# Where a step of a sliding-window attention copies the next query, and what stands ahead of it

## The chip, the core and the metric

The kernel runs on one core of one Trainium2 chip, in float32 throughout, with the matrix products split into high and low parts. The metric is the device time of one execution in microseconds (us), lower being better. Five engines work side by side and each takes its instructions strictly in the order in which they were issued: TensorE (PE in the profile; its weight loads are PEld), VectorE (DVE), ScalarE (ACT), GpSimd (POOL) and SyncE (SP), which issues nearly all DMAs. What one engine needs from another it waits for by a semaphore, and everything queued behind a waiting instruction on the same engine waits with it.

## The reference

Four layers with a residual each, on one sequence of 2048 rows of 640 values: attention, Fourier mixing, attention, Fourier mixing. An attention layer has 32 heads of 20 values; each row looks at 8 rows, itself and every second one before it. Cut to what matters:

```python
def _A_ref(x, wqkv, wo):                     # H = 32, Dh = 20, W, dil = 8, 2
    qkv = (x @ wqkv).reshape(B, S, 3, H, Dh).transpose(2, 0, 3, 1, 4)
    q, k, v = qkv[0], qkv[1], qkv[2]
    idx = pos[:, None] - arange(W)[None, :] * dil            # masked where < 0
    logits = einsum("bhsd,bhswd->bhsw", q, k[idx]) * Dh ** -0.5
    attn = softmax(where(mask, logits, -1e9))
    o = einsum("bhsw,bhswd->bhsd", attn, v[idx])
    return o.transpose(0, 2, 1, 3).reshape(B, S, D) @ wo

x = x + _A_ref(layernorm(x), wqkv, wo)
x = x + Real(DFT_seq(DFT_hidden(layernorm(x))))              # as matrix products
x = x + _A_ref(layernorm(x), wqkv, wo)
x = x + Real(DFT_seq(DFT_hidden(layernorm(x))))
```

## The kernel before, in words

`layer_a` is one attention layer and runs twice; `LayerB` is a Fourier layer. This case is about `layer_a`. The sequence is cut into 4 chunks c of 512 rows (128 partitions of 4 rows j), the heads into 8 groups e of 4 heads. A unit u = (c, e), 32 of them, is one head group on one chunk. A window of 8 rows and 20 values per head is too small for TensorE, so logits and weighted sums are made elementwise on VectorE and GpSimd, while TensorE makes the q, k, v projections of the following chunk, the output projections of the chunk before, and the first products of the Fourier layer.

The layer is written as steps, two to a unit: unit u's two halves (jp = 0 and 1, two rows each) start in the even step 2u and the odd step 2u + 1. A helper `at(step, phase, fn)` files every piece of work under a step and a phase name; at the end the list `PHASES` gives the order of the phases inside a step, and all pieces are issued in that order, for all five engines at once and without any other scheduler. So `PHASES` alone decides who stands behind whom on an engine within a step. Different phases may hold work of different engines; only the order among those of one engine, and the waits between engines, matter.

The pieces that matter here, by step:

- `qk` (`qk_mul`, L421 on DVE and L423 on POOL), each step: products of query and window, 128x1280 values, then POOL adds the two halves of each head.
- `red0`, `red1` (`qk_red`, L429 on DVE): the rest of the logit sum, one step after its `qk`. `red0` is the second half's and falls into even steps, `red1` the first half's and falls into odd steps.
- `qc` (`q_copy`, L394 on ACT), odd steps: copies the next unit's query from the landed tile `qs` into `qp`, in PSUM. There is one `qp`.
- `sA`, `sB`, `sC` (L444, L446, L448 on DVE), then `exp` (L437 on ACT), in even steps: mask, maximum, subtraction, exponential of the unit before.
- `sD`, `sE`, `sF` (L450, L452, L454 on DVE), odd steps: sum, reciprocal, and the probabilities `pp`.
- `av0`, `av1` (`av_mul`, L459 on DVE; `av_tree`, L474 to L476 on POOL): probability times value window, and a tree of adds. `av0` falls into even, `av1` into odd steps.
- ACT also empties the projections' PSUM banks: `evac`, `evacA`, `evacO` (L359), splits transposed tiles into high and low parts (`hi` L321, `actL` L340), and does `actl`: normalisation of x (L172, L181), its statistics (L141 to L160, first layer), output statistics (L154 to L160), the high part of wo (L550), the Fourier layer's input (L181, L843).
- PE: transposes (`peT0`, L317), projections (`pe`, `pe2`, L352), subtraction of the high part (`peL`, L325), output projections (L499), Fourier products (`pe3`, L886).
- POOL: `fin`, the reciprocal root of a variance (L164, L166). SP: `dma` with the query's load (`q_load`, L386, L391) and `dma2` with loads for the Fourier layer (L185, L485, L486).

`qp`, the probabilities `pp`, the maximum `mx`, the sum `sm` and the mask all are parts of one PSUM tile `pq` (2 KB a partition). Waits are made for the tile as a whole, so the query copy waits for the last access of VectorE to any part of it that was issued ahead of the copy, and a later write of VectorE to `sm` waits for the copy.

```python
        pq = pt([P, 512], "pq")
        qp = pq[:, : NJ * FE].rearrange("p (j f) -> p j f", j=NJ)
```

Of the kernel before, what the change touches and what calls it, by code (L numbers as in the profile page):

```python
# [71 lines left out]
def tile_layers(ctx: ExitStack, tc: tile.TileContext, x, wqkv, wo, cs, wre, wim, out):  # L72
# [159 lines left out]
    def layer_a(li, stats, handoff, prev):  # L232
# [545 lines left out]
        for z in range(len(thirds) // 3):  # L778
# [8 lines left out]
        at(63, "misc", handoff.c_lo, 13)  # L787

        PHASES = (
            "peT0 dma evac hi pe peL pe2 fin red0 dma2 qk sA sB av0 sD red1 sE sC exp evacA actL evacO actl sF av1 qc"  # L790
            " dmaw dmas misc dmac dmar pe3w pe3"
        ).split()
        with tc.manual_schedule(engines=ENGINES):
# [425 lines left out]
    st0 = [None] * NC  # L1219
    b1, b2 = LayerB(1), LayerB(3)  # L1220
    layer_a(0, st0, b1, None)
    st2 = [None] * NC
    b1.run(st2)
    layer_a(2, st2, b2, b1)
    b2.run(None)
    b2.ytile(NT - 1, 0, None)
# [56 lines left out]
```

## Time and profile before

| | us |
|---|---|
| median of 3 runs | 1844.46 |
| lowest and highest run | 1843.17, 1844.85 |
| the profiled execution | 1844.03 |
| its span, first to last instruction | 1842.2 |

| engine | busy us | share of the span |
|---|---|---|
| PE | 1762.7 | 96% |
| DVE | 1443.5 | 78% |
| ACT | 821.8 | 45% |
| POOL | 716.4 | 39% |

The two attention layers take, roughly, 30 to 370 us and 950 to 1310 us of the span. How to read the rows: a group's row has the line, engine, operation, tiles, count, then busy time and the mean of one in ns, then the idle time of the engine just ahead of the group and what ended most of it. A row of the timeline has the start in us from the span's start, the duration, the engine, the line and the tiles, and in brackets how long the engine was idle ahead of it and who released it. A row of the windows has, for each stretch, the busy time of PE, PEld, DVE, ACT and POOL, then the granted TensorE clock, the share of the DMA engines and the rate in GB/s. A row of the waits has who waited for whom, the total, the number of times and the longest.

### The profile page before, as it was taken

How to read it: one execution, taken by the hardware profiler on the slowest of the kernel's cores; microseconds unless marked ns; L12 is line 12 of the kernel's file. 1: busy time of each engine (PE TensorE's matmuls, PEld its weight loads, DVE VectorE, ACT ScalarE, POOL GpSimd, SP SyncE). 2: the span in 40 equal slices, each digit the busy share in tenths (PEclk: the TensorE clock that was granted, in tenths of full speed). 3: DMA queues.
4: the chain of work that ended last, by engine and by line, in shares of the span. 5: the costliest groups of instructions: out<-in, count | busy, mean ns of one | idle time of the engine just before them, and what ended most of it. 6: DMA issues, size and time to landing. Idle time of an engine off the chain costs nothing.

```text
span 1842.2 us, 26541 instructions
## 1 busy us (share of the span) xinstructions
PE 1762.7 (96%) x8798; PEld 1517.6 (82%) x8798; DVE 1443.5 (78%) x2158; ACT 821.8 (45%) x1713; POOL 716.4 (39%) x637
## 2 busy tenths in 40 slices
PE   9999997988999999999998999988889999999999
PEld 7789896767788888888897798977678888888888
DVE  5899899989867767767649988898798676676673
ACT  5554544553445444445624334445533443443441
POOL 4799898954200000000028987889441000000000
PEclk9999998999999999999999999989999999999999
DMA  6766677656777687676646665775477776876861
GB/s 232 227 188 212 190 229 240 208 173 230 246 261 242 207 272 234 221 261 220 190 145 220 217 198 180 218 263 187 158 248 246 262 242 205 273 238 217 262 216 51
DMA packets 261722, 401.89 MB, mean 218 GB/s; under 512 B 21808, under 2 KB 146224, under 8 KB 261328
## 3 DMA queue, kind: packets, MB, share of 16 engines
q1 hardware_dynamic: 258384, 398.22, 66.9%
q10 hardware_dynamic: 3200, 1.97, 0.3%
q8 instruction: 70, 1.15, 0.3%
q14 instruction: 68, 0.56, 0.1%
HBM read 326.63 MB, written 73.47 MB: 217 GB/s over the span
## 4 chain that ended last, share of the span: by engine, by line
PE 66%; DVE 16%; DMA 5%; issue 5%; POOL 5%; ACT 3%; SPq 0%; DVEq 0%; ACTq 0%; POOLq 0%
PE m L352 15%; PE aux L964 12%; PE t L1054 10%; PE m L1054 10%; PE pq L1054 5%; PE xt L1054 5%; PE aux L499 5%; DVE pr L421 3%; DVE pr L459 2%; DMA win<-cs_in 1%; POOL pr L474 1%; DVE s L1016 1%; DVE s L1017 1%; DVE lg L429 1%; POOL pr L423 1%
## 5 line engine op out<-in xcount | busy, mean ns | idle before, releaser
L352 PE MATMUL m<-r,s 128*128 128x480 f32 x1920 | 442.0, 385 | 9.7 <-ACT stg L359 4.2
L352 PEld LDWEIGHTS m<-r,s 128*128 128x128 f32 x1920 | 358.0, 190 | 67.0 <-ACT stg L359 6.5
L1047 ACT CAST r<-win 128x512 fp32r<-128x512 f32 x242 | 147.9, 621 | 176.6 <-DVE win L1083 91.4
L964 PE MATMUL aux<-r2a,zo 128*128 128x320 f32 x768 | 226.3, 309 | 0.0
L474 POOL TENSOR_TENSOR pr<-pr 128x640 f32<-128x640 f32 x126 | 205.0, 1627 | 49.9 <-DVE pr L459 49.3
L164 POOL TENSOR_TENSOR stats<-stats,mhalf 128x1 f32<-128x1 f32 (+1 forms) x40 | 27.6, 689 | 490.0 <-ACT stats L160 489.9
L421 DVE TENSOR_TENSOR pr<-pq,win 128x1280 f32<-128x1280 f32 x128 | 189.8, 1483 | 33.0 <-ACT pq L394 33.0
L964 PE MATMUL aux<-pr,zo 128*128 128x320 f32 x704 | 208.0, 309 | 0.0
L1048 DVE TENSOR_TENSOR r<-win,r 128x512 fp32r<-128x512 f32 x242 | 162.6, 687 | 42.1 <-ACT r L1047 40.9
L459 DVE TENSOR_TENSOR pr<-pq,win 128x1280 f32<-128x1280 f32 x128 | 190.9, 1491 | 4.5 <-DVE pq L454 0.2
L423 POOL TENSOR_TENSOR pr<-pr 128x640 f32<-128x640 f32 x128 | 184.7, 1443 | 19.7 <-DVE pr L421 16.3
L1054 PE MATMUL m<-r,r 128*128 128x512 f32 x600 | 154.5, 392 | 0.0
L886 PE MATMUL m<-s,r 128*128 128x512 f32 x384 | 123.7, 410 | 27.2 <-DVE s L871 13.9
L964 PEld LDWEIGHTS aux<-r2a,zo 128*128 128x128 f32 x768 | 144.1, 188 | 2.0
L964 PEld LDWEIGHTS aux<-pr,zo 128*128 128x128 f32 x704 | 132.2, 188 | 2.2
L1054 PE MATMUL t<-r,r 128*128 128x512 f32 x492 | 133.5, 393 | 0.0
L1054 PEld LDWEIGHTS m<-r,r 128*128 128x128 f32 x600 | 112.5, 188 | 25.1 <-DVE r L1048 0.3
L886 PE MATMUL t<-s,r 128*128 128x512 f32 x384 | 121.8, 405 | 2.5 <-DVE ot L943 2.0
L475 POOL TENSOR_TENSOR pr<-pr 128x320 f32<-128x320 f32 x126 | 118.7, 942 | 9.9
L886 PEld LDWEIGHTS m<-s,r 128*128 128x128 f32 x384 | 71.3, 193 | 51.0 <-DVE s L871 20.1
L359 ACT COPY stg<-m 128x480 f32<-128x480 f32 x128 | 71.0, 556 | 94.9 <-PE m L352 85.0
L1083 DVE TENSOR_TENSOR win<-win,win 128x512 f32<-128x512 f32 x109 | 74.9, 690 | 47.6 <-DMA win<-cs_in 46.2
(271 smaller groups left out, 3455.7 us busy)
## 6 DMA issues: line engine op xcount, KB each, us to landing
win<-cs_in SPq DMA_DIRECT2D x348, 256.0 KB, 3.9
r<-xc SPq DMA_DIRECT2D x240, 256.0 KB, 4.2
win<-kvb SPq DMA_DIRECT2D x96, 440.0 KB, 3.9
xa<-cs_in SPq DMA_DIRECT2D x120, 256.0 KB, 3.7
win<-kvb SPq DMA_DIRECT2D x64, 360.0 KB, 4.2
xc<-stg SPq DMA_DIRECT2D x40, 512.0 KB, 3.6
kvb<-stg SPq DMA_DIRECT2D x60, 320.0 KB, 4.3
xr<-xs SPq DMA_DIRECT2D x40, 320.0 KB, 3.1
```

The lines of the kernel that those rows point to most:

```text
L352: nc.tensor.matmul(mt[g][:, : 3 * F], st[:, a, k], wq[q][:, b, k], start=n == 0, stop=n == 14)
L421: nc.vector.tensor_tensor(pr, q, wview(u, jp, 0, [[1, FE]]), op=ALU.mult)
L423: nc.gpsimd.tensor_tensor(pv[:, :, 0:10], pv[:, :, 0:10], pv[:, :, 10:20], op=ALU.add)
L459: nc.vector.tensor_tensor(pr.rearrange("p j w (h d) -> p j w h d", d=DH), lgs[u][:, 2 * jp : 2 * jp + 2].unsqueeze(4).to_broadcast([P, 2, ...
L474: g.tensor_tensor(pr[:, :, 0:4], pr[:, :, 0:4], pr[:, :, 4:8], op=ALU.add)
L475: g.tensor_tensor(pr[:, :, 0:2], pr[:, :, 0:2], pr[:, :, 2:4], op=ALU.add)
L499: nc.tensor.matmul(m[:, :320], oT[(c, j)][:, a, k], wo_s["w"][:, b, k, e * 320 : (e + 1) * 320], start=(i, k) == (0, 0), stop=(i, k) == (2 ...
L886: self.last = nc.tensor.matmul(self.z[t][k], self.xn[c][:, a, j, k * P : (k + 1) * P], self.ct[s][:, b], start=s == 0 and i == 0, stop=s = ...
L964: self.last = nc.tensor.matmul(self.ym[e][:, :320], zt[(k, a, ri)][:, j2 * P : (j2 + 1) * P], w[:, e * 320 : (e + 1) * 320], start=(k, a, ...
L1047: nc.scalar.copy(hi, raw)
L1048: nc.vector.tensor_tensor(lo, raw, hi.bitcast(F32), op=ALU.subtract)
L1054: nc.tensor.matmul(bank, w(a, kb), hl[b], start=start and (a, b) == (0, 0), stop=stop and (a, b) == (1, 0),)
```

## The change

Only the order of the phases changes. `red0`, `dma2`, `qk`, `qc` and `red1` go to the head of the step, in that order; the rest keeps its order.

```diff
         PHASES = (
-            "peT0 dma evac hi pe peL pe2 fin red0 dma2 qk sA sB av0 sD red1 sE sC exp evacA actL evacO actl sF av1 qc"
+            "red0 dma2 qk qc red1 peT0 dma evac hi pe peL pe2 fin sA sB av0 sD sE sC exp evacA actL evacO actl sF av1"
             " dmaw dmas misc dmac dmar pe3w pe3"
         ).split()
```

No instruction is added or removed. Engine by engine, in the order in which they are issued:

- PE: nothing moves.
- DVE: in each odd step the logit sum L429 (`red1`) goes ahead of the sum L450 (`sD`). Nothing else moves.
- ACT: in each odd step the query copy L394 goes from the end of the step to its beginning: ahead of `evac`, `hi`, `evacO` and `actl` of that step, but still behind all of the even step before. The copy now follows the second query product of its step and no longer the probability product (L459).
- POOL: `fin` goes behind L423 of the same step.
- SP: the query's load goes behind the loads of `dma2`, on 12 steps.
- Waits: the copy's target is in `pq`, so L450, which is issued behind the copy now, waits for it, and the first query product of the next unit (L421) has no wait for ScalarE left.

## The prediction

> **What bounds the kernel now.** I read the page first, then the busy time by stretches, then the table of waits, and last the timeline of single steps.
>
> ```profile
> PE 1762.7 (96%) x8798; PEld 1517.6 (82%) x8798; DVE 1443.5 (78%) x2158; ACT 821.8 (45%) x1713; POOL 716.4 (39%) x637
> ...
> L421 DVE TENSOR_TENSOR pr<-pq,win 128x1280 f32<-128x1280 f32 x128 | 189.8, 1483 | 33.0 <-ACT pq L394 33.0
> ```
>
> PE is busy nearly throughout, but as an average over stages. The second row is what the change is about: 128 products, two to a query copy, and VectorE stood 33.0 us in all ahead of them. The stretches of the two attention layers tell where that can count:
>
> ```profile
> 75.00:113.00 38.00, 33.88 (x142) 27.52 (x140) 36.57 (x46) 15.10 (x38) 31.62 (x29) 0.91 0.61 195
> 113.00:225.00 112.00, 111.63 (x590) 99.53 (x591) 101.99 (x142) 62.57 (x163) 102.04 (x98) 1.00 0.67 207
> 225.00:285.00 60.00, 59.01 (x320) 52.76 (x318) 54.37 (x83) 27.79 (x67) 56.26 (x52) 1.00 0.72 221
> 285.00:362.00 77.00, 63.80 (x312) 55.20 (x313) 70.26 (x100) 37.61 (x91) 69.59 (x62) 0.91 0.67 220
> ...
> 1036.00:1180.00 144.00, 144.00 (x765) 129.04 (x764) 123.89 (x178) 60.76 (x152) 122.86 (x113) 1.00 0.65 206
> 1180.00:1290.00 110.00, 96.40 (x501) 84.75 (x501) 97.84 (x145) 52.56 (x128) 100.32 (x88) 0.94 0.68 220
> ```
>
> From 113 to 225 and from 1036 to 1180 PE has next to no gap (111.63 of 112, 144 of 144): there a VectorE that waits costs nothing until the stretch ends. In 75 to 113 VectorE is busy 36.57 of 38 us and PE only 33.88: VectorE leads. From 225 on VectorE and GpSimd carry the end of the layer together (54.37 and 56.26 of 60, then 70.26 and 69.59 of 77), while PE has 13 to 14 us of gaps in each last stretch. So the change is worth what it does to VectorE and GpSimd where they take over from PE, about 225 and 1180, and what it does to PE where PE takes over, about 113 and 1016.
>
> ```profile
> ACT pq L394 <- DVE pr L459: 37.4, 21, 4.7
> DVE pr L421 <- ACT pq L394: 33.0, 21, 4.8
> ```
>
> The copy waited 37.4 us for the probability product, with all later work of ScalarE behind it; that goes. VectorE's 33.0 us came in 21 places. The Trainium skill ("Perfetto Trace Analysis", Optimization Strategy) says that a gap which repeats for a stretch can mean too few SBUF or PSUM buffers for the next tile. By it the gap would not go away here, since there is still one query buffer; the rival of no change below is what that would make.
>
> **The wait that takes its place.** In the changed order the sum L450 is a write to the copy's PSUM tile that stands behind the copy, and so waits for it; the next unit's L421 no longer does. The copy itself has left behind the ScalarE work of its own odd step, but not that of the even step: bank eviction, low parts, normalisation for the Fourier layer. VectorE therefore meets the copy about 3.7 us earlier in its own list (L450, L452, L454, L459 and a logit sum come after the new place and came before the old). The pair of steps at 1178 shows it:
>
> ```profile
> 1178.60 1.49 DVE L421 TENSOR_TENSOR pr<-pq,win 128x1280 f32<-128x1280 f32 x1
> 1179.10 0.32 ACT L437 ACTIVATE lg<-lg 128x128 f32<-128x128 f32 x1
> 1180.18 0.38 DVE L450 TENSOR_REDUCE pq<-lg 128x16 f32<-128x128 f32 x1
> 1180.48 0.81 DVE L429 TENSOR_REDUCE lg<-pr 128x64 f32<-128x640 f32 x1
> 1181.20 0.26 DVE L452 RECIPROCAL pq<-pq 128x16 f32<-128x16 f32 x1
> 1181.49 0.29 DVE L454 TENSOR_TENSOR pq<-lg,pq 128x128 f32<-128x128 f32 x1
> 1181.82 1.49 DVE L459 TENSOR_TENSOR pr<-pq,win 128x1280 f32<-128x1280 f32 x1
> 1181.97 0.56 ACT L359 COPY stg<-m 128x480 f32<-128x480 f32 x1 [2.55 <-PE m L352]
> 1182.43 0.76 ACT L340 CAST ot<-t 128x256 fp32r<-128x256 f32 x2
> 1183.06 0.94 ACT L181 ACTIVATE xa<-xa,stats 128x640 f32<-128x640 f32 x1
> 1183.39 1.58 POOL L474 TENSOR_TENSOR pr<-pr 128x640 f32<-128x640 f32 x1 [1.17 <-DVE pr L459]
> 1184.04 0.73 ACT L843 CAST r<-xa 128x640 fp32r<-128x640 f32 x1
> 1186.07 0.42 ACT L394 COPY pq<-qs 128x320 f32<-128x320 f32 x1
> 1186.52 1.49 DVE L421 TENSOR_TENSOR pr<-pq,win 128x1280 f32<-128x1280 f32 x1 [2.48 <-ACT pq L394]
> ```
>
> L359, L340, L181 and L843 are of the even step and stay ahead of the copy; L359 there waits for a projection on PE. L843 ends at 1184.77, so the copy runs 1184.79 to 1185.21 (0.9 us earlier than now), L450 starts at 1185.24, L452 at 1185.65 instead of 1181.20: 4.45 later. L421 loses its wait of 2.48. Net the next unit starts 4.45 - 2.48 = 1.97 us later, and L474 on GpSimd, released by L459, 4.4 later, where it had 1.17 of idle time. Queued behind the waiting L450 is all of VectorE's step; GpSimd waits for that.
>
> Where ScalarE has only short work ahead of the copy, the move is free: the copy needs 0.06 + 0.42 + 0.03 = 0.5 us from the end of the step's L421 (gaps between neighbouring rows), and L429, now ahead of L450, covers it with 0.72 (1180.48 to 1181.20). The cover is gone once ScalarE is over 0.2 us late. Such pairs are most.
>
> **Leaving PE's stretch, layer one.**
>
> ```profile
> 223.61 1.49 DVE L421 TENSOR_TENSOR pr<-pq,win 128x1280 f32<-128x1280 f32 x1
> 226.24 0.26 DVE L452 RECIPROCAL pq<-pq 128x16 f32<-128x16 f32 x1
> 227.94 0.79 ACT L340 CAST ot<-t 128x256 fp32r<-128x256 f32 x2
> 230.46 1.49 DVE L421 TENSOR_TENSOR pr<-pq,win 128x1280 f32<-128x1280 f32 x1 [1.39 <-ACT pq L394]
> ...
> 246.75 0.25 DVE L452 RECIPROCAL pq<-pq 128x16 f32<-128x16 f32 x1
> 247.56 0.73 ACT L843 CAST r<-xa 128x640 fp32r<-128x640 f32 x1
> 250.04 1.49 DVE L421 TENSOR_TENSOR pr<-pq,win 128x1280 f32<-128x1280 f32 x1 [0.46 <-ACT pq L394]
> ```
>
> The same working: L340 ends at 228.73, the copy at 229.17, L452 starts at 229.6 instead of 226.24, 3.37 late, less 1.39: 1.98. At 247 L843 ends at 248.29, L452 would start at 249.17: 2.4 late, less 0.46. That is 1.96 by itself, but a VectorE that already is 2.0 late finds the first part of ScalarE's list done. Laid behind its exponential, the list (0.32, 0.56, 0.76, 0.94, 0.73 and the copy's 0.42, less 0.1 of overlap between neighbours) takes about 3.2 against 2.2 for L421 and L429: about 1 us more. Later pairs with a normalisation in the even step would cost 1 us each again, but GpSimd is the later one there. Sum: 3.1 late (2.0 + 1.1). Layer two: 1.97 at 1178 and, by the same list, 1.5 in the pair behind it: 3.5.
>
> **What comes back.** In the ends of the layers some waits lie behind work that the copy does leave (odd steps' casts, statistics, normalisation):
>
> ```profile
> 345.52 1.49 DVE L421 TENSOR_TENSOR pr<-pq,win 128x1280 f32<-128x1280 f32 x1 [0.82 <-ACT pq L394]
> 1247.38 1.49 DVE L421 TENSOR_TENSOR pr<-pq,win 128x1280 f32<-128x1280 f32 x1 [1.32 <-ACT pq L394]
> ```
>
> 0.8 in layer one, 1.3 in layer two.
>
> **Where PE takes over.**
>
> ```profile
> 113.78 1.48 DVE L421 TENSOR_TENSOR pr<-pq,win 128x1280 f32<-128x1280 f32 x1
> 114.00 0.93 ACT L181 ACTIVATE xa<-xa,stats 128x640 f32<-128x640 f32 x1
> 116.70 0.60 PE L317 MATMUL xt<-ident,xa 128*128 128x128 f32 x4
> ...
> 1010.26 1.48 DVE L421 TENSOR_TENSOR pr<-pq,win 128x1280 f32<-128x1280 f32 x1
> 1015.04 0.43 ACT L394 COPY pq<-qs 128x320 f32<-128x320 f32 x1 [5.21 <-issue]
> 1015.41 0.55 ACT L359 COPY stg<-m 128x480 f32<-128x480 f32 x1
> 1016.01 2.37 PE L352 MATMUL m<-r,s 128*128 128x480 f32 x8 [2.32 <-ACT stg L359]
> ```
>
> At 113.78 the copy now stands ahead of an eviction and of the normalisation L181, and waits for L421's end at 115.26. Copy, eviction and bias behind it, L181 ends at about 117.45; the transposes that started at 116.70 start 0.8 later. At 1016 the opposite: ScalarE stood 5.21 us at the copy with an eviction behind it for which PE waited 2.32. The copy can now run at 1011.8, and these 2.32 go; but a normalisation that moves behind the copy soon after takes most of it back, by the row at 114. Bounds 0 and 2.32 of gain; I take 0.4, nearer to the lower, since VectorE leads up to there.
>
> **What moves at no cost.** PE's order does not change. On VectorE L450 and L452 become neighbours that depend on each other: 0.02 a pair (0.38 + 0.03, and 0.72, against 1.1 now), 1.2 us over 62 pairs if all were on the path, under half of it. The Trainium skill ("VectorE: DVE Perf Modes", The DRAIN you can't avoid) says that a semaphore between chained operations costs nothing extra: 0 by it; I take 0. On GpSimd the 0.55 us roots (L164) go behind L423; their reader is a step later, so nothing waits; without that cover 0.55 each. On SP the query's load goes behind up to two loads of `dma2` on 12 steps; it can be issued a pair of steps ahead of its use, and without that cover costs its place in the queue.
>
> **Sum.** +0.8 + 3.1 - 0.8 - 0.4 + 3.5 - 1.3 = +4.9 us on the profiled execution's 1844.03 (1842.2 of span and 1.8 around): 1848.9. The median of the runs is 0.4 above that execution: 1849.4.
>
> **Rivals.** Changes under 0.2% (3.7 us) could hardly be told from none.
>
> No change, 1844 to 1848: the later start is taken up by waits of VectorE for PE's output projections in the layers' ends, and what comes back meets the rest. For it: VectorE and GpSimd have about 7 of 77 us idle there. Against: those waits follow PE, which there follows VectorE. Chance 0.26.
>
> Faster, 1838: ScalarE's standing at the copy was the real loss. Place: evictions and high parts behind the copy, such as the one at 1016. If PE keeps the 2.32 there and gets as much in layer one, with 0.8 and 1.3 coming back and the lag swallowed, that is -6 to -7. It decides if L450 finds the copy done at 1181 to 1185, which needs ScalarE's even list to end sooner than its rows do. Chance 0.16.
>
> Much slower, 1862: normalisations behind the copy hold the transposes not once but at each of 24 tiles, 0.8 each (18 us), once VectorE runs late inside PE's stretches. Against: there VectorE waits for PE, so its L421 is done early. Chance 0.10; the forecast has 0.48.
>
> **How the numbers follow.** Slower by over 0.2%: 0.48 + 0.10 = 0.58; within: 0.26; faster: 0.16. The unknown bounds (0 to 2.32 at two places, 1 us a pair in each layer's end, 1.2 for L450) make the forecast's own range 1844 to 1854. For eight in ten it reaches towards both outer rivals: 1839.5 to 1857.
>
> **What would show it.** L421's waits for L394 all but gone (33.0 to under 3); in their place L450 waiting for L394, 30 to 50 us in all, with over 4 us at 1181; ScalarE's wait of L394 on L459 gone, on L421 instead; GpSimd idle longer ahead of L474. Wrong, if L450 hardly waits, if PE's busy time between 113 and 225 falls by more than 1 us, or if the layers' ends are no later than now.

## The result, and the profile after

| | before | changed |
|---|---|---|
| median, us (17 runs each) | 1843.99 | 1847.09 |
| lowest and highest run | 1840.44, 1846.75 | 1844.27, 1850.71 |
| ratio of the times, with its 95% interval | | 1.0018 [1.0010, 1.0025] |
| the profiled execution, and its span | 1844.03, 1842.2 | 1850.71, 1848.5 |

The change costs 3.3 us (1.8 to 4.6 by the interval; here and below the us beside a ratio are worked out from it on 1844.5): slower, by an interval that leaves out no change. The prediction of 1849.4 was 2.3 us high. The profiled execution of the changed kernel is its slowest of 17, 6.7 us from that of before, so the 3.3 us must not be read from the spans; the same instructions are compared by place further down.

Page of the changed kernel: busy times and two groups.

```profile
PE 1766.7 (96%) x8798; PEld 1521.1 (82%) x8798; DVE 1442.0 (78%) x2158; ACT 820.9 (44%) x1713; POOL 712.8 (39%) x637
...
L474 POOL TENSOR_TENSOR pr<-pr 128x640 f32<-128x640 f32 x126 | 204.8, 1625 | 64.2 <-DVE pr L459 64.0
...
L421 DVE TENSOR_TENSOR pr<-pq,win 128x1280 f32<-128x1280 f32 x128 | 189.5, 1482 | 2.3 <-ACT stg L359 1.5
```

Busy times are those of before within 4 us an engine. The product L421 has lost its 33.0 us of waiting for the copy. What it costs instead stands in the waits of the changed kernel (who waited for whom, total, times, longest):

```profile
POOL pr L474 <- DVE pr L459: 64.0, 39, 5.1
...
DVE pq L450 <- ACT pq L394: 43.8, 27, 4.0
...
ACT pq L394 <- DVE pr L421: 18.4, 14, 3.1
```

VectorE now waits 43.8 us for the copy at the sum L450, more than the 33.0 it was spared. Where that matters is seen in the timeline of the changed kernel at the end of PE's stretch in layer one, and the same in layer two:

```profile
221.53 1.49 DVE L421 TENSOR_TENSOR pr<-pq,win 128x1280 f32<-128x1280 f32 x1
...
222.93 0.81 DVE L429 TENSOR_REDUCE lg<-pr 128x64 f32<-128x640 f32 x1
...
225.47 0.56 ACT L359 COPY stg<-m 128x480 f32<-128x480 f32 x1 [2.30 <-PE m L352]
...
226.56 0.79 ACT L340 CAST ot<-t 128x256 fp32r<-128x256 f32 x2
227.19 0.49 ACT L394 COPY pq<-qs 128x320 f32<-128x320 f32 x1
...
227.71 0.39 DVE L450 TENSOR_REDUCE pq<-lg 128x16 f32<-128x128 f32 x1 [3.97 <-ACT pq L394]
...
228.14 0.27 DVE L452 RECIPROCAL pq<-pq 128x16 f32<-128x16 f32 x1
...
230.34 1.57 POOL L474 TENSOR_TENSOR pr<-pr 128x640 f32<-128x640 f32 x1 [5.01 <-DVE pr L459]
...
1185.02 0.56 ACT L359 COPY stg<-m 128x480 f32<-128x480 f32 x1 [2.56 <-PE m L352]
...
1186.12 0.94 ACT L181 ACTIVATE xa<-xa,stats 128x640 f32<-128x640 f32 x1
...
1187.09 0.73 ACT L843 CAST r<-xa 128x640 fp32r<-128x640 f32 x1
1187.73 0.42 ACT L394 COPY pq<-qs 128x320 f32<-128x320 f32 x1
...
1188.18 0.39 DVE L450 TENSOR_REDUCE pq<-lg 128x16 f32<-128x128 f32 x1 [3.89 <-ACT pq L394]
```

The product is done at 223.0, the copy could run then; but ScalarE still has the eviction L359 of the even step to do, which itself waits 2.30 for PE, and the low part L340. The copy runs at 227.19, VectorE stands idle 3.97 us ahead of the sum, and GpSimd 5.01 us ahead of its additions. That is the mechanism that the prediction worked out, at both of its places.

**By place.** PE's and VectorE's instructions are the same and nearly all in the same order in all kernels below, so each can be compared with itself. The table gives how much later (us, each counted from the start of its own span) the PE instructions of a stretch of 10 us start than in the profiled execution of before (median of the stretch that begins at the head of the column; VectorE's at 1280, where PE has gaps). The first row is the changed kernel; the others are the experiments that follow, without the three that store values elsewhere.

| kernel | 20 | 100 | 210 | 290 | 400 | 820 | 940 | 1060 | 1160 | 1220 | 1280 | 1320 |
|---|---|---|---|---|---|---|---|---|---|---|---|---|
| changed | -0.19 | -1.70 | -1.35 | 2.36 | 1.52 | 1.24 | 3.69 | 3.04 | 3.05 | 6.04 | 5.12 | 6.18 |
| changed order to step 35 | -0.06 | -1.70 | -1.34 | -1.22 | -1.69 | -2.18 | 0.13 | 1.10 | 1.10 | 0.82 | 0.51 | -0.94 |
| changed order from step 36 | -0.06 | -0.08 | 0.01 | 3.71 | 3.08 | 2.98 | 2.08 | 2.21 | 2.22 | 5.00 | 4.24 | 4.18 |
| copy moved alone | 0.00 | 0.12 | 2.13 | 8.63 | 9.36 | 9.45 | 8.25 | 10.18 | 10.19 | 15.24 | 15.62 | 14.15 |
| all but the copy moved | -0.11 | -0.30 | -0.25 | -0.39 | -1.22 | -2.62 | -3.90 | -4.12 | -4.12 | -4.31 | -3.25 | -4.68 |
| copies at the exits on VectorE | -0.07 | -1.68 | -1.36 | 1.04 | 0.40 | 0.26 | 0.89 | 0.26 | 0.26 | 0.83 | 0.51 | -0.61 |
| changed order to 35 and from 54 | -0.07 | -1.73 | -1.39 | -1.32 | -0.84 | -1.68 | -2.92 | -2.04 | -2.04 | -2.04 | -3.30 | -4.83 |
| changed order to step 11 | -0.09 | -1.75 | -1.63 | -1.60 | -2.00 | -2.20 | 0.44 | -0.17 | -0.17 | -0.13 | -1.24 | -1.15 |
| changed order to 11 and from 54 | 0.01 | -1.63 | -1.51 | -1.54 | -2.45 | -1.99 | -1.69 | -2.27 | -2.27 | -2.28 | -2.68 | -3.76 |
| the same, between them all but the copy moved | 0.03 | -1.62 | -1.71 | -1.85 | -3.01 | -2.71 | -3.33 | -4.26 | -4.26 | -4.46 | -4.59 | -5.69 |

A step from one column to the next is what that stretch adds. Between 400 and 940 lies the Fourier layer, whose code no kernel changes: there single executions drift by up to 2.7 us either way. In the changed kernel the PE instructions fall back by 2.44 between 880 and 930 us, and the windows show a lower granted TensorE clock there (the third figure from the end of a row), first in the trace of before, then in that of the changed kernel:

```profile
880.00:930.00 50.00, 46.59 (x265) 41.88 (x264) 28.56 (x54) 26.48 (x55) 0.00 (x0) 1.00 0.55 168
```

```profile
880.00:930.00 50.00, 47.03 (x249) 41.68 (x248) 30.10 (x55) 26.97 (x55) 0.00 (x0) 0.93 0.52 162
```

So of the 6.3 us between the two spans about 4.2 belong to the attention layers (1.71 and 2.49), which fits the 3.3 of the medians within its interval; the rest lies where no code was changed.

### The profile page after: what moved, and what is told of

Its sections match the earlier page's. It is cut to its first block, busy times and chain, and to the rows that moved or that the text cites. A ratio compares the mean times of both kernels' runs of the same rounds, so it can differ in the third digit from the quotient of the medians.

```text
span 1848.5 us, 26411 instructions
## 1 busy us (share of the span) xinstructions
PE 1766.7 (96%) x8798; PEld 1521.1 (82%) x8798; DVE 1442.0 (78%) x2158; ACT 820.9 (44%) x1713; POOL 712.8 (39%) x637
## 3 DMA queue, kind: packets, MB, share of 16 engines
q8 instruction: 70, 1.15, 0.3%
## 4 chain that ended last, share of the span: by engine, by line
PE 67%; DVE 16%; POOL 6%; DMA 5%; issue 4%; ACT 2%; SPq 0%; DVEq 0%; ACTq 0%; POOLq 0%
PE m L352 16%; PE aux L964 13%; PE t L1054 10%; PE m L1054 10%; PE pq L1054 5%; PE xt L1054 5%; PE aux L499 4%; DVE pr L421 2%; DVE pr L459 2%; POOL pr L474 2%; DMA win<-cs_in 1%; POOL pr L423 1%; DVE s L1016 1%; DVE s L871 1%; DVE lg L429 1%
## 5 line engine op out<-in xcount | busy, mean ns | idle before, releaser
L474 POOL TENSOR_TENSOR pr<-pr 128x640 f32<-128x640 f32 x126 | 204.8, 1625 | 64.2 <-DVE pr L459 64.0
L459 DVE TENSOR_TENSOR pr<-pq,win 128x1280 f32<-128x1280 f32 x128 | 190.9, 1491 | 4.6 <-DVE pq L454 0.2
L421 DVE TENSOR_TENSOR pr<-pq,win 128x1280 f32<-128x1280 f32 x128 | 189.5, 1482 | 2.3 <-ACT stg L359 1.5
L423 POOL TENSOR_TENSOR pr<-pr 128x640 f32<-128x640 f32 x128 | 185.0, 1446 | 10.8 <-DVE pr L421 10.0
L475 POOL TENSOR_TENSOR pr<-pr 128x320 f32<-128x320 f32 x126 | 117.1, 930 | 9.9
L429 DVE TENSOR_REDUCE lg<-pr 128x64 f32<-128x640 f32 x128 | 103.8, 811 | 15.8 <-POOL pr L423 15.5
L359 ACT COPY stg<-m 128x480 f32<-128x480 f32 x128 | 70.8, 553 | 101.0 <-PE m L352 86.1
```

Source lines behind the costliest of these rows:

```text
L421: nc.vector.tensor_tensor(pr, q, wview(u, jp, 0, [[1, FE]]), op=ALU.mult)
L423: nc.gpsimd.tensor_tensor(pv[:, :, 0:10], pv[:, :, 0:10], pv[:, :, 10:20], op=ALU.add)
L429: nc.vector.tensor_reduce(lgs[u][:, 2 * jp : 2 * jp + 2].rearrange("p j w h -> p (j w h)"), prq.pop((u, jp))[:, :, 0:10], axis=AX.X, op=AL ...
L459: nc.vector.tensor_tensor(pr.rearrange("p j w (h d) -> p j w h d", d=DH), lgs[u][:, 2 * jp : 2 * jp + 2].unsqueeze(4).to_broadcast([P, 2, ...
L474: g.tensor_tensor(pr[:, :, 0:4], pr[:, :, 0:4], pr[:, :, 4:8], op=ALU.add)
L475: g.tensor_tensor(pr[:, :, 0:2], pr[:, :, 0:2], pr[:, :, 2:4], op=ALU.add)
```

## The experiments

The theory: the change has two halves. Before PE's stretch the copy's earlier place frees ScalarE's eviction behind it (a gain); at the exits of PE's stretches the new wait of L450 for a copy behind ScalarE's list delays VectorE (a loss, larger). The rivals: the entry loses as predicted or its gain is swallowed; the work moved beside the copy, not the copy, makes the loss.

**1 and 2. The change cut by steps.** One half keeps the new list below step 36, the other from step 36 on, in both attention layers.

```diff
-                for ph in PHASES:
+                for ph in EARLY if s < 36 else LATE:     # EARLY new, LATE old; and the other way round
```

> The changed order in the steps up to 35, the old order from step 36 on (the last steps of PE's stretch, the end of layer one, all later layers). Theory 1 (my terms, by place): the loss is made where the layers' ends begin, so this half keeps only the entry of layer one. The two traces lie 1.2 us apart in the changed kernel's favour from about 90 us on until PE's stretch ends, where I had predicted a loss of 0.8. If that gain is real it lasts: 1841 to 1843, 1 to 2.5 us under before, and VectorE waits next to nothing for the copy before 230 us. Theory 2 (rival: the early difference is swallowed, since the end of layer one is led by VectorE and GpSimd, whatever PE has gained by 225): 1843.5 to 1844.5, no difference. Theory 3 (the entry term as predicted, +0.8): 1844.8.

Measured: 1842.67, ratio 0.9986 [0.9974, 0.9998], 2.6 us faster than before. In its trace VectorE waits 24.9 us for the copy ahead of the sum, 8.2 of them before 225 us, where next to nothing was expected. Of the 24.9, 17.8 lie inside PE's stretches, where they cost little (100 to 210: +0.36, 1060 to 1160: 0.00); the exits at 290 and 1220 add nothing. Layer two's entry, which the expectation left out, adds 0.97 (940 to 1060):

```profile
DVE pq L450 <- ACT pq L394: 24.9, 13, 4.0
```

> The counterpart: the old order in the steps up to 35, the changed one from step 36 on. Theory 1 (by place): exits of both layers and the regains only, +3.1 - 0.8 - 0.4 + 3.5 - 1.3 = +4.1 by the prediction, +4 to +5 by the two traces: 1848 to 1849.5, more than the whole change (3.3). Theory 2 (the early difference is swallowed): the same as the whole change, 1847 to 1847.6. In the trace VectorE's waits for the copy ahead of the sum start at about 225 us.

Measured: 1848.97, ratio 1.0023 [1.0014, 1.0032], +4.2 us. Its row in the table is level with before to 210, then +3.7 and +2.8 at the exits. The halves lie where theory 1 put them: a gain before the stretch, a loss at the exits, and the gain of the first half lasts. Together they make +1.6, in line with the 3.3 of the whole within the intervals.

**3 and 4. Other storage, so that the sum has nothing to wait for.**

```diff
-        mx = pq[:, o : o + NJ * HE].rearrange("p (j h) -> p j h", j=NJ)
-        sm = pq[:, o + NJ * HE : o + 2 * NJ * HE].rearrange("p (j h) -> p j h", j=NJ)
+        mx = sm = T([P, NJ, HE], "mx")                          # SBUF
...
-                v.tensor_tensor(pp, lg, sm.unsqueeze(2).to_broadcast([P, NJ, W, HE]), op=ALU.mult)
-                lgs[u] = pp
+                v.tensor_tensor(lg, lg, sm.unsqueeze(2).to_broadcast([P, NJ, W, HE]), op=ALU.mult)
```

> The changed order, and other storage: the maxima and the sums get a small tile of their own in SBUF instead of the copy's PSUM tile, and the probabilities are written over the exponentials in the logit tile. So the sum and the probability scaling no longer wait for the copy; the copy waits for nothing but the query products. Theory 1 (the new wait of the sum for the copy is the loss): the waits of 43.8 us go, the layers' ends start as early as before or earlier, and what L421 no longer waits (33.0) counts: 1838 to 1843 and at least 4 us under the changed kernel. Theory 2 (rival: the order of the neighbouring work is the loss: normalisations and evictions behind the copy, roots behind the tree on GpSimd): 1846 to 1848, as the changed kernel. The storage alone is the next kernel.

> The storage of the kernel just above (maxima and sums in a tile of their own, probabilities over the exponentials) in the old order. It is the control: here the copy, though issued after the probability product, no longer has to wait for it. If theory 1 is right that the shared PSUM tile and not the order makes the loss, this one and the one above lie within 1.5 us of each other, both at 1838 to 1843. If only the order matters, this one lies at 1843.5 to 1844.5 and the one above at 1846 to 1848. A cost or gain of reading SBUF instead of PSUM in the scaling would show in both.

Measured: 1949.55, ratio 1.0568 [1.0551, 1.0585], and in the old order 1951.1, ratio 1.0574 [1.0557, 1.0591]. Every theory missed by over 100 us: the edit brought in a cost of its own, so the two tell nothing of the wait. Groups of the first (changed order; its lines from 455 on are one lower: L458 is the probability product, L473 to L475 are GpSimd's tree):

```profile
L458 DVE TENSOR_TENSOR pr<-lg,win 128x1280 f32<-128x1280 f32 x128 | 235.1, 1836 | 2.3 <-DVE lg L454 0.2
...
L423 POOL TENSOR_TENSOR pr<-pr 128x640 f32<-128x640 f32 x128 | 221.0, 1727 | 11.3 <-DVE pr L421 10.7
...
L475 POOL TENSOR_TENSOR zo<-pr 128x160 f32<-128x160 f32 x126 | 144.7, 1149 | 9.9
...
L448 DVE TENSOR_TENSOR lg<-lg,mx 128x128 f32<-128x128 f32 x64 | 59.3, 927 | 0.1
```

The same operations on the same shapes, with both operands now in SBUF (`lg` and `win`, `lg` and `mx`, in place of one in `pq`), take 1836 ns against 1491, and 927 against 278; and GpSimd's additions, not touched at all, take 1727 against 1443 and 1149 against 543. Run 10 takes this apart.

**5. The copy moved, the logit sum not.** The head of the step is the new one, but `red1` stays behind `sD`.

```diff
-"red0 dma2 qk qc red1 peT0 dma evac hi pe peL pe2 fin sA sB av0 sD sE ..."
+"red0 dma2 qk qc peT0 dma evac hi pe peL pe2 fin sA sB av0 sD red1 sE ..."
```

> The changed order, but the odd step's logit sum L429 stays where it was, behind the softmax sum L450: the copy is moved, and the sum that waits for it has no L429 ahead of it as cover. Theory 1 (the copy's new place is the whole of the change: it gives the early gain of 2 and makes the loss at the ends): at least the changed kernel's loss, plus up to 0.7 in the pairs where the sum waits a little: 1846.5 to 1850. Theory 2 (rival: what is moved beside the copy, the logit sum above all, makes the loss): 1841 to 1843.5, only the early gain left.

Measured: 1861.41, ratio 1.0089 [1.0073, 1.0105], +16.4 us, in theory 1's direction and far over its range. Its waits:

```profile
DVE pq L450 <- ACT pq L394: 73.8, 60, 4.6
```

60 waits against 27. The L429 that the change puts between product and sum covers 0.72 us of each; for the other 33 that was enough. Without it the sum waits in nearly every pair, the early gain is gone (0.12 at 100 in the table; run 9 shows where), and the two exits add 6.5 and 5.05 us. So moving `red1` along is what makes the change cost 3.3 and not 16.

**6. All that the change moves, except the copy.**

```diff
-"red0 dma2 qk qc red1 peT0 ... sF av1"
+"red0 dma2 qk red1 peT0 ... sF av1 qc"
```

> The complement: all that the change moves except the copy, which stays behind the probability product. Theory 1: no wait of the sum for the copy, and the copy waits for the product as before, so neither gain nor loss: 1843.5 to 1845.5, with L421 waiting some 30 us for the copy. Theory 2 (the rest makes the loss): 1846 to 1848.

Measured: 1843.2, ratio 0.9989 [0.9979, 0.9998]: 2.0 us under before, by an interval that barely leaves out no change; theory 2 falls. The waits are those of before:

```profile
ACT pq L394 <- DVE pr L459: 37.2, 21, 4.7
...
DVE pr L421 <- ACT pq L394: 34.7, 21, 4.9
```

In the table it is level with before to 290 us; most of its lead arises between 400 and 940, outside the attention layers. The profiled execution is this kernel's fastest of 11 (1839.41), so its lead at the end is not that of the median.

**7. The copies at the exits on VectorE.** If the copy is late only because of what stands ahead of it on ScalarE, another engine can do it in time.

```diff
         def q_copy(u):
-            nc.scalar.copy(qp, qs[u])
+            if u in ((19, 20) if first else (23, 24)):
+                nc.vector.tensor_copy(qp, qs[u])
+            else:
+                nc.scalar.copy(qp, qs[u])
```

> The changed order, with two copies in each layer (steps 37 and 39 of layer one, 45 and 47 of layer two, where VectorE leaves PE's stretch) done by VectorE itself in place of ScalarE, so that the sum there doesn't stand behind ScalarE's list. Each costs VectorE about 0.4 us. Theory 1 (the ends are lost because the copy stands behind ScalarE's evictions, high parts and normalisations): of the 3.9 and 3.0 that the ends lose, about 2 to 2.5 and 1.5 to 2 come back: 1842 to 1844. Theory 2 (the neighbours' order makes the ends late): 1846.5 to 1848, the copies' cost on top.

Measured: 1843.27, ratio 0.9997 [0.9986, 1.0008]: the loss is gone. Timeline of this kernel (its lines are three higher: L395 is VectorE's copy, L397 ScalarE's, L453 the sum, L846 the Fourier input):

```profile
223.04 0.49 DVE L395 COPY pq<-qs 128x320 f32<-128x320 f32 x1
...
224.17 0.38 DVE L453 TENSOR_REDUCE pq<-lg 128x16 f32<-128x128 f32 x1
...
246.16 0.73 ACT L846 CAST r<-xa 128x640 fp32r<-128x640 f32 x1
246.79 0.42 ACT L397 COPY pq<-qs 128x320 f32<-128x320 f32 x1
...
247.25 0.39 DVE L453 TENSOR_REDUCE pq<-lg 128x16 f32<-128x128 f32 x1 [3.04 <-ACT pq L397]
```

For 0.4 us of VectorE the sum starts at 224.17 where it started at 227.71. The exits add 2.40 and 0.57 us instead of 3.71 and 2.99; what is left in layer one is the next copy, still ScalarE's, behind the normalisation and L846: 3.04 us. This shows that the place in ScalarE's list makes the loss.

**8. The changed order at both ends, the old one in steps 36 to 53.**

```diff
-                for ph in PHASES:
+                for ph in MIDDLE if 36 <= s < 54 else ENDS:     # MIDDLE old, ENDS new
```

> The changed order up to step 35 and again from step 54 on, the old order in steps 36 to 53: entry and regain without the exits. By the terms measured so far: -2.0 for the early half, -1.0 and -1.0 for the regains at about 340 and 1250 us: 1840 to 1842, under both kernels. If the regain only gives back time that VectorE lost by the change itself (rival), it is not there after the old order: 1842 to 1843.5.

Measured: 1841.36, ratio 0.9984 [0.9974, 0.9995], -3.0 us: faster than either kernel. Against run 1 it is 0.4 us better by the ratios, within the intervals; the medians don't tell whether the regain is there after the old order. The two traces differ by layer: the end of layer one gains nothing here (+0.48 from 290 to 400, against -0.47 in run 1), that of layer two gains more (-2.79 from 1220 to 1320, against -1.76). As these are single executions, it stays open.

**9. The changed order in steps up to 11 alone.**

```diff
-                for ph in PHASES:
+                for ph in EARLY if s < 12 else LATE:     # EARLY new, LATE old
```

> The changed order in the steps up to 11 alone, the old order from step 12 on, in both layers. Theory 1 (the early gain of layer one is one place: at 86 us the old copy waited 3.1 us for the probability product, with the eviction and the high parts behind it for which PE waited 2.6): the trace runs some 1.3 to 1.7 us ahead of before from 90 us on and keeps that to the end of layer one; the time 1842 to 1843.5. Theory 2 (the gain is built up over the steps to 35): the trace is level with before at 120 us, 1844 to 1845.

Measured: 1843.06, ratio 0.9991 [0.9982, 0.9999], -1.7 us. The table has -1.75 at 100 and keeps it to 290 (-1.60): the early gain of layer one arises in these steps. Theory 1 names a place for it. The timeline there, first of before, then of the changed kernel:

```profile
86.28 0.43 ACT L394 COPY pq<-qs 128x320 f32<-128x320 f32 x1 [3.13 <-DVE pr L459]
...
87.10 0.59 ACT L321 CAST s<-xt 128x512 fp32r<-128x512 f32 x1
...
87.74 0.50 PE L325 MATMUL xt<-s,nident 128*128 128x512 f32 x1 [2.56 <-ACT s L321]
...
92.33 3.17 PE L352 MATMUL m<-r,s 128*128 128x480 f32 x7 [0.66 <-ACT s L340]
```

```profile
81.46 0.43 ACT L394 COPY pq<-qs 128x320 f32<-128x320 f32 x1
...
84.93 0.59 ACT L321 CAST s<-xt 128x512 fp32r<-128x512 f32 x1
...
85.58 0.50 PE L325 MATMUL xt<-s,nident 128*128 128x512 f32 x1 [0.59 <-ACT s L321]
...
90.67 4.65 PE L352 MATMUL m<-r,s 128*128 128x480 f32 x13 [2.30 <-ACT s L340]
```

In the old order ScalarE stood 3.13 us at the copy, waiting for the probability product, with the high parts L321 behind it, and PE waited 2.56 for those. Now PE waits 0.59 and starts 2.2 us earlier. But most of this is given back at once: at the next wait, for the low part L340, PE stands 2.30 us where it stood 0.66. ScalarE makes L340 behind the exponential L437, which waits for VectorE. VectorE leads here, and what lasts is the 1.65 us by which VectorE is earlier. It won 1.40 of them in one instruction, the subtraction L553 for the low part of wo, whose two operands both lie in SBUF. Before, then the changed kernel:

```profile
79.35 1.57 POOL L474 TENSOR_TENSOR pr<-pr 128x640 f32<-128x640 f32 x1 [0.71 <-DVE pr L459]
79.38 2.22 DVE L553 TENSOR_TENSOR r2a<-zo,r2a 128x640 fp32r<-128x640 f32 x1
```

```profile
79.21 0.82 DVE L553 TENSOR_TENSOR r2a<-zo,r2a 128x640 fp32r<-128x640 f32 x1
...
79.41 2.06 POOL L474 TENSOR_TENSOR pr<-pr 128x640 f32<-128x640 f32 x1
```

In the old order L553 starts 0.03 us behind a GpSimd addition and takes 2.22 us; in the changed one it starts 0.20 ahead of it and takes 0.82, and the addition takes 2.06 instead of 1.57. GpSimd had been made late by the new wait of L450 (1.77 us) one pair earlier. The profiles agree: where the copy has its old place in these steps (before, runs 2 and 6) this L553 takes 2.22 us and there is no early gain; in all other kernels of the table it takes 0.82 to 0.93. In run 5 PE starts 1.98 us earlier at 87.74 as well, but VectorE loses what it won at L553 in the next three pairs, where L450 waits 0.50 to 0.57 us for the copy, and in the column at 100 nothing is left. So the early gain comes in the main of which of the two engines starts first, and not of the list behind the copy. This is read from the traces; no run moves L553 alone.

**10. Only the maxima and sums in SBUF, in the changed order.**

```diff
-        mx = pq[:, o : o + NJ * HE].rearrange("p (j h) -> p j h", j=NJ)
-        sm = pq[:, o + NJ * HE : o + 2 * NJ * HE].rearrange("p (j h) -> p j h", j=NJ)
+        mx = sm = T([P, NJ, HE], "mx")                          # SBUF
```

> The changed order with only the maxima and sums in a small SBUF tile of their own; the probabilities stay in the copy's PSUM tile. The sum and the reciprocal no longer wait for the copy, the scaling behind them (write to the PSUM tile) still does: VectorE has 0.7 us more of its own work ahead of the wait. Theory A (the 105 us of the two storage kernels came from the products L459, which there read both operands from SBUF): the product takes 1.49 us again as a mean and GpSimd's additions 1.44 and 1.63; the time is near the changed kernel, by up to 4 us better: 1843 to 1847. Theory B (the small tile in SBUF, read by many short operations, made it): 1900 or more.

Measured: 1853.67, ratio 1.0049 [1.0036, 1.0063], +9.0 us. Theory A holds for the product and fails for the time: the short operations have a price too. Groups of this kernel:

```profile
L459 DVE TENSOR_TENSOR pr<-pq,win 128x1280 f32<-128x1280 f32 x128 | 190.2, 1486 | 2.5 <-DVE pq L454 0.4
...
L448 DVE TENSOR_TENSOR lg<-lg,mx 128x128 f32<-128x128 f32 x64 | 43.4, 678 | 0.1
...
L454 DVE TENSOR_TENSOR pq<-lg,mx 128x128 f32<-128x128 f32 x64 | 28.3, 442 | 32.8 <-ACT pq L394 28.2
...
L444 DVE TENSOR_TENSOR lg<-lg,pq 128x128 f32<-128x128 f32 x32 | 8.9, 277 | 0.0
```

The product, again with one operand in PSUM, is back at 1486 ns. L448 and L454, now with two in SBUF, take 678 and 442 against 278 and 296, while the mask addition L444, of L448's shape with one operand in PSUM, keeps its 277. That is (0.40 + 0.146) x 64 = 35 us more of VectorE. What the sum's earlier start is worth stays hidden behind it.

**11 and 12. Keeping what gains.** The changed order in steps up to 11 and from 54 on; between them the old order, or all of the change but the copy.

```diff
-                for ph in PHASES:
+                for ph in MIDDLE if 12 <= s < 54 else ENDS:     # ENDS new; MIDDLE old, or that of run 6
```

> The changed order in the steps up to 11 and from step 54 on, the old order between. Theory 1 (two kinds of place gain: the eviction held behind the old copy before PE's stretch, and the regains where the layers end; the normalisation behind the new copy at 1031 us and the waits of the sum at the exits lose): no transposes held for 1.84 us at 1031, no sum waiting 4 us at the exits: 1839.5 to 1841.5, as good as or up to 1.5 us better than the changed order in steps up to 35 and from 54 on (0.9984 of before). Theory 2 (the entry of layer two doesn't count): as that one, 1841 to 1843.

> The kernel just above, with one difference: in the steps 12 to 53 all that the change moves is moved, except the copy. If the rest of the change by itself gains (its time was 0.9989 of before, its trace level with before to 300 us), it shows here as 1 to 2 us under the kernel above; if that was the scatter of the Fourier layers' stretches, the two agree within 1 us.

Measured: 1840.09, ratio 0.9979 [0.9969, 0.9989], and 1840.11, ratio 0.9977 [0.9966, 0.9987]: 3.9 and 4.2 us under before. They agree, so the rest of the change has no gain of its own that shows in this place; why run 6 came out at -2.0, with an interval that ends at 0.9998, stays open. In the first of them VectorE hardly meets the copy at the sum:

```profile
DVE pq L450 <- ACT pq L394: 8.8, 8, 2.2
```

Between runs 8 and 11 the table differs most in the stretch of layer two's entry (940 to 1060): +0.88 us with the changed order up to step 35, -0.58 with it up to step 11 alone; by the ratios (0.9984 and 0.9979) the two are not apart. Runs 11 and 12 have the lowest medians of all.

## Why the prediction was right, step by step

| step of the sum | predicted | measured in the profiled executions |
|---|---|---|
| entry of PE's stretch, layer one | +0.8 | -1.51 to 100 us, +0.35 to 210: -1.2 |
| its exit | +3.1 | +3.71 |
| regain | -0.8 | -0.84 |
| entry, layer two | -0.4 | -0.64 |
| its exit | +3.5 | +2.99 |
| regain | -1.3 | -0.92, and +1.06 behind it (1280 to 1320) |
| sum | +4.9 | +4.2, by the medians 3.3 |

The +1.06 at the very end of layer two stays open: of the other kernels with the changed order there, none shows it (run 2: -0.06).

**How near the number is, and why.** The sum is 0.7 us from the measured one because its errors cancel: the entry of layer one was 2.0 too high, the end of layer two 1.4 too low, the exits 0.6 too low and 0.5 too high. That is luck; the two exits are not, since each came out near its own working. By its size, 0.18%, the result also lies in the range that the prediction gave to its rival of no change (1844 to 1848), so the time alone doesn't decide between them; the places and runs 2 and 7 do.

**What held.** The exits carry the loss, by the wait that was named: L450 for L394 43.8 us (predicted 30 to 50), L421 2.3 with nothing of it for the copy (under 3), the copy waiting for L421 and no longer for L459, GpSimd's idle time ahead of L474 up from 49.9 to 64.2, PE's busy time between 113 and 225 not lower (below). At the first exit the working put L452 at 229.6; it came at 228.14 in a stretch that ran 1.35 us early, so within 0.2. Runs 2 and 7 show it by experiment. The wait at 1188 was 3.89 where over 4 was named: the list ahead of the copy was as listed. The windows of the changed kernel:

```profile
113.00:225.00 112.00, 111.96 (x591) 99.43 (x590) 101.07 (x141) 62.95 (x162) 102.14 (x99) 1.00 0.67 211
225.00:285.00 60.00, 57.77 (x310) 51.06 (x310) 51.50 (x76) 27.30 (x67) 51.48 (x48) 1.00 0.65 207
```

Between 225 and 285 VectorE does 51.50 us of work where it did 54.37, and GpSimd 51.48 against 56.26: that is the stretch that starts late.

**What failed: the entry of layer one,** +0.8 forecast and -1.2 measured. The step priced ScalarE's list alone: as loss the normalisation L181 ahead of the transposes, as gain PE's 2.32 at 1016. The loss is there and is small: the transposes start at 115.14, right behind L181, which ends at 115.09, and PE falls back by 0.20 there. What the step left out is the engine that the prediction itself had named as leading in this stretch, VectorE, and an instruction of it whose length is not fixed. The trace of before has L553 at 0.81 to 2.22 us, and the change turned one of them from 2.22 into 0.82 (run 9). That worth of 1.4 us came of the order in which two engines happened to start, which nothing in the prediction worked out. The wait of PE behind the copy at 87.74, the same pattern as at 1016, was not counted either; it went, but most of it came back at 92.33.

The rival of a faster kernel held ScalarE's standing at the copy for the real loss. Its waits did go, in layer one as in layer two, but run 5 has the earlier start at 87.74 too and no gain at 100; and the rival's condition failed, since L450 did not find the copy done at the exits.

**The entry of layer two** came out near its number, and PE's 2.32 at 1016 is gone as written. An eviction (1.69 at 1023.13) and a normalisation take it back. But here too one L553 fell from 2.22 to 0.92 us (at 986.32 in before), against new waits of VectorE for the copy, and VectorE gained 0.65 over the stretch, as much as PE. So that the two parts of the step make the -0.64 is not shown. Timeline of the changed kernel, with PE held by the L181 that now stands behind the copy:

```profile
1033.61 0.43 ACT L394 COPY pq<-qs 128x320 f32<-128x320 f32 x1 [0.68 <-ACT stg L359]
...
1034.00 0.92 ACT L181 ACTIVATE xa<-xa,stats 128x640 f32<-128x640 f32 x1
...
1034.97 0.66 PE L317 MATMUL xt<-ident,xa 128*128 128x128 f32 x4 [1.85 <-ACT xa L181]
```

**The rival of no change** had the loss taken up by waits for PE in the layers' ends. It was not: the changed order from step 36 on still has 3.1 of its 3.7 us at 400. The Trainium skill's rule on gaps that repeat ("Perfetto Trace Analysis", Optimization Strategy), weighed there, agrees in so far as the gap didn't go away with one query buffer: 33.0 us became 43.8; that this leaves the time alone, the runs don't bear out, and run 7 took the loss away with no buffer added. The rival of a much slower kernel, in which the normalisations hold the transposes at every tile, did not come either: all of PE's waits for L181 at L317 come to 3.4 us in two places, against 1.5 in one before. (24 times 0.8 is 19.2 and not the 18 written there.)

**Moved at no cost.** This held for the whole (run 6: no loss), but one such move was worth far more than was said: the L429 that goes ahead of the sum. The prediction had its cover (0.72) and that 0.5 is enough where ScalarE has only short work ahead of the copy; run 5 shows the price without it, 13 us more (1.0089 against 1.0018).

## What to carry to other kernels

When an instruction is moved up on an in-order engine, list for each place where it waited both what stands ahead of its new place (that is its new lateness) and what stood behind its old one (that is freed), and follow each to the engine that leads in that stretch; time won on another engine lasts only as far as the leader is earlier too, as PE's 2.0 us at 87.74 show. Then look for instructions whose shortest and longest executions differ, as L553's 0.81 and 2.22: a new order shifts which engine starts first, and such a shift was worth as much as a term of the sum. Where stretches differ, an order that may change with the step can beat one order for all: here the change kept in the first and last steps was 0.21% faster than before where the change as a whole was 0.18% slower. And when a new wait can't be avoided, put independent work of the waiting engine ahead of it: one 0.72 us reduction was worth 13 us.

## What the runs showed of the hardware that was not expected

A VectorE operation with two tensor operands in SBUF takes longer while GpSimd is at work, and so does GpSimd. Timeline of run 3:

```profile
159.22 0.87 POOL L474 TENSOR_TENSOR pr<-pr 128x320 f32<-128x320 f32 x1
159.32 2.11 DVE L458 TENSOR_TENSOR pr<-lg,win 128x1280 f32<-128x1280 f32 x1
...
160.16 1.66 POOL L475 TENSOR_TENSOR zo<-pr 128x160 f32<-128x160 f32 x1
```

VectorE's product began beside a running GpSimd addition and took 2.11 us instead of 1.49; the next GpSimd addition, 0.54 us in the kernel before, took 1.66 and ended at 161.82, 0.39 us after the product. All products of run 3 bear it out: the 22 that began with no GpSimd instruction at work took 1.47 to 1.49 us, the 106 that began beside one 1.47 to 2.86. In the kernel before, where one operand lies in PSUM, 113 of the 128 began beside one too and all took 1.48 or 1.49. The Trainium skill ("SBUF — State Buffer", Who interferes with whom) says that a VectorE instruction with two SBUF inputs contends with a GpSimd instruction that reads SBUF, over a shared read interface; that the shared ports are an exclusive lock, where the order of issue decides who blocks; and that at most one SBUF input does not contend. These rows agree with it, and so do the 277 to 278 ns of the short operations with one operand in PSUM against 678 and 927. In this kernel that placement is worth over 100 us (1.0568 and 1.0574), some thirty times the change under study. The profile before pointed to it: L553, the same instruction on the same shape, took 0.81 to 0.82 us four times, 0.87 and 1.42 once each, and 2.19 to 2.22 four times; each of these last four began beside a GpSimd addition with some 1.5 us still to go.
